# All DMA transposes issued by ScalarE instead of SyncE, and a new order of all instructions

## The chip, the cores and the metric

The kernel runs on one core of a Trainium2 chip. A core has five engines with a queue of instructions each: TensorE (PE, matmuls into PSUM), VectorE (DVE), ScalarE (ACT, activations and copies), GpSimd (POOL) and SyncE (SP, which here issues DMAs). They share on-chip memory (SBUF), and 16 DMA engines move the data. The queues run side by side and wait for each other on semaphores. A DMA is issued by an instruction in the queue of one engine. The metric is the time of one execution on the device in microseconds; the median of the runs counts.

## The reference

Attention with a choice of key chunks by bounds, then a gated MLP with a mix over the sequence (batch B = 4, heads H = 8, sequence S = 768, head size 64, model size 512, hidden size 1024):

```python
k_min, k_max = min and max of k over chunks of 32 keys
ub = sum_d max(q * k_min, q * k_max)              # bound of each (query, chunk)
ub = where(query's chunk >= chunk, ub, -1e9)
sel = the 6 chunks with the largest ub
scores = where(sel and key <= query, q @ k.T / 8, -1e9)
attn_out = softmax(scores) @ v                    # heads joined: x, (4, 768, 512)
h = gelu_tanh(x @ w_in);  u, v = halves of h
v_n = (v - mean) / sqrt(var + 1e-6) * g_ln
v_s = einsum('ts,bsd->btd', w_sg, v_n) + b_sg
out = x + (u * v_s) @ w_out
```

(The first, third and fourth lines are put shortly here.)

## The kernel before

The 32 heads go in 16 pairs, p = 0 to 15; four pairs make a batch b, and after its four pairs a batch goes through the MLP. Everything is unrolled, and every step is recorded by `P.op(engine, function, cost, tag, ...)` with what it reads and writes.

For each pair, `kside` (pairs 0 to 9) or `kside_full` (pairs 10 to 15) readies the keys. The first transposes the keys `kn` on PE and evicts them (`kev`) into `KA`. The second reduces `kn` to the chunk bounds on DVE (L580), casts the two heads of the pair into the tile `kbx` (`kcast`, POOL or ACT; for odd pairs this tile is `IND`, so that the page shows `kbx` and `IND`), and transposes each head by DMA into `KA` (`kT_p_i`, L587). `qside` transposes the queries on PE, evicts them to `qT` (`qev`), makes the positive part `rT` (`rel`) and casts `QA` (`qcast`). `vside` casts the values. `select` and `select_full` compute the bounds (`ub`), pick the chunks and write the mask `Dt`, which SP copies into `QA` (`qd`, L742). `scores` and `scores_full` multiply `KA` by `QA` into one of the two double banks `PSC` (`sc`, L778), and ACT takes the exponential into `E` (`exp_p_i_c`, L784, three pieces for each head). `head` multiplies `E` by the values (`pv`, `pvd`) and DVE scales the result into `XS` (`xs`, L873).

When two heads of `XS` are there, `xtrans(b, dk)` puts their transpose into `xT`: for batches 1 and 2 by DMA (`dt_x_b_dk`, L882), for 0 and 3 on PE with an eviction (`xev`). `moe_h` multiplies `xT` by `w_in`; ACT takes GELU into `vgb` (`gv`, L909) and `uT` (`gu`, L950); DVE takes statistics and forms `vhat`. `moe_g` mixes over the sequence (L962), gates on DVE, and multiplies by `w_out` (L981); DVE adds `XS` into `osb` and SP stores it (L992).

The exponential and GELU need different activation tables, so ACT's list has one block of GELUs for each batch, with a table load on each side.

The order on each engine is written out: `TABLE` holds, for each engine, the numbers of its recorded steps in the order in which they are issued, the PSUM bank of each tile (`slots`), and the engine of the steps that can go to more than one (`engine`, read into `ENG` by tag). The cost tuples, `dmac(1250)` for one, are a planner's, and the planner is not in the file; the emitted program does not depend on them. `place` puts the lists in place. `link` finds for each step the semaphore waits that its data needs and that no earlier step of the same engine has waited for. An engine issues in order, so that a step that waits holds all later ones of its list. A DMA in a list waits, is issued, and its landing raises a semaphore of its own.

In the kernel before every DMA is in SP's list (158 steps), the 20 transposes among them: 12 `kT` (pairs 10 to 15, two heads each) and 8 `dt_x` (batches 1 and 2, four each).

Of the kernel before, what the change touches and what calls it, by code (L numbers as in the profile page):

```python
# [261 lines left out]
def _build(nc, ctx, q, k, v, w_in, g_ln, w_sg, b_sg, w_out, out):  # L262
# [30 lines left out]
    P = Program()  # L293
# [47 lines left out]
    xT = [T(f"xT{i}", [128, NDK, S], BF16) for i in range(2)]  # L341
# [83 lines left out]
    ENG = dict(x.split(":") for x in TABLE["engine"].split())  # L425
# [68 lines left out]
    QRUN = [0] * 16  # L494
    KRUN = [0] * 16
# [80 lines left out]
    def kside_full(p, u, x):  # L576
# [7 lines left out]
        for i in range(2):  # L584
            flex("pool", ("act",), lambda i=i: kbx[n][:, i, :, 64 * i:64 * i + 64], lambda i=i: kn[s][:, i], TG + 60,
                 ("kcast", p, i), [("kn", s, 0), ("kn", s, 1), ("kbi", n, i)], [("kbx", n, i)])
            P.op("sp", lambda e, i=i: e.dma_start_transpose(  # L587
                KA[w][i][:].rearrange("p (t x) -> p t x", x=128), kbx[n][:, i].rearrange("p t c -> p (t c)")), dmac(1250),
                ("kT", p, i), reads=[("kbx", n, i), ("kbi", n, i)], writes=[("KA", w, i, 0), ("KA", w, i, 1), ("KI", w, i)],
                dma=f"kT{w}_{i}", xfer=900)  # L590
# [287 lines left out]
    def xtrans(b, dk):  # L878
        src = XS[:, b % 2, dk]
        rd = [("XS", b % 2, 2 * dk), ("XS", b % 2, 2 * dk + 1)]  # L880
        if (b, dk) in DXT:
            P.op("sp", lambda e: e.dma_start_transpose(xT[b % 2][:, dk, :].rearrange("p (t x) -> p t x", x=128),  # L882
# [3 lines left out]
        t = ps_g.tile((0, 1))  # L886
# [160 lines left out]
    for p in range(4, NP + 4):  # L1047
# [37 lines left out]
    "act": (  # L1085
# [10 lines left out]
    "dve": (  # L1096
# [17 lines left out]
    "pool": (  # L1114
# [12 lines left out]
    "slots": (  # L1127
        "23102213010323200101101110130011110010232110001110123120310010010032011111010102300110103332323232322232"
# [73 lines left out]
```

## Time and profile before

| | |
|---|---|
| runs of the kernel before | 220.44, 222.28, 221.87 us; median 221.87 |
| the profiled execution | 220.88 us, its span 218.8 us |
| granted TensorE clock | 1.000 |
| DMA | 36.27 MB in 98,235 packets, mean 166 GB/s |
| SP waiting | longest in total: L992 for DVE osb, 30.8 us in 10 times |

The span runs from the first to the last instruction. Busy time counts computing only: issuing a DMA is an instruction of its engine's queue, but not busy time. In a row of groups stand the line, engine, operation, output and inputs with the shape, the count, then the busy time and the mean ns of one, then the idle time just before and what ended it. In a row of waits stand the waiting engine, tile and line, what it waited for, and the total in us, the times and the longest. SPq is SP's queue.

### The profile page before, as it was taken

To read this page: it belongs to the slowest core of one execution; us is meant where nothing else is said; L and a number is where in the kernel's file an instruction comes from. 1 tells how busy PE (TensorE), PEld (TensorE's weight loads), DVE (VectorE), ACT (ScalarE), POOL (GpSimd) and SP (SyncE) were. 2 spreads that over 40 slices of the span, in tenths; PEclk is the share of its full clock that TensorE was granted. 3 is DMA by queue.
4 is the path that set the end of the run, shared out by engine and by line. 5 is a ranking of instruction groups with operands and counts; after the bars stand their busy time and mean duration, and the time that the engine had idled before them with its cause. 6 is when DMAs were issued, how large, how long until landed. Compare 5 with 4: busy or idle time off the path is not lost.

```text
span 218.8 us, 5980 instructions
## 1 busy us (share of the span) xinstructions
PE 199.7 (91%) x2363; PEld 131.0 (60%) x2377; DVE 187.1 (85%) x532; ACT 166.6 (76%) x251; POOL 93.5 (43%) x132
## 2 busy tenths in 40 slices
PE   7599999989999997987996999998898999999992
PEld 3366676846757575666563667776444668555550
DVE  4899999899999998898989988956888768968993
ACT  3979999988999999788879867987867788275000
POOL 7333946991359743346124443796114034002000
PEclk9999999999999999999999999999999999999999
DMA  7999999993999979896999798985944004001216
GB/s 153 252 220 216 212 241 349 345 226 71 223 223 259 215 180 248 190 151 126 178 176 227 178 217 126 236 128 76 182 103 115 3 0 147 3 0 48 96 61 230
DMA packets 98235, 36.27 MB, mean 166 GB/s; under 512 B 92448, under 2 KB 93216, under 8 KB 98208
## 3 DMA queue, kind: packets, MB, share of 16 engines
q1 hardware_dynamic: 98208, 35.89, 76.7%
q8 instruction: 19, 0.31, 0.6%
q14 instruction: 8, 0.07, 0.1%
HBM read 24.77 MB, written 6.29 MB: 142 GB/s over the span
## 4 chain that ended last, share of the span: by engine, by line
PE 55%; DVE 25%; DMA 9%; issue 3%; POOL 3%; SPq 2%; ACT 2%; DVEq 0%
PE PSG L962 15%; PE PSC L778 9%; PE PSG L981 8%; PE PSG L524 5%; PE PSG L856 4%; DVE vhat L933 4%; DVE Wall L563 3%; DVE stats L914 3%; DMA kn<-in_k_dram 3%; PE PSG L905 3%; PE PSG L945 2%; PE PSG L709 2%; DMA QA<-Dt 2%; DMA out_dram<-osb 2%; PE PSG L863 2%
## 5 line engine op out<-in xcount | busy, mean ns | idle before, releaser
L784 ACT ACTIVATE E<-PSC 128x1024 bf16<-128x1024 f32 (+1 forms) x72 | 62.7, 916 | 13.8 <-PE PSC L778 13.3
L778 PE MATMUL PSC<-QA,KA 128*128 128x128 bf16 (+2 forms) x336 | 36.5, 246 | 1.7 <-DMA QA<-Dt 1.3
L962 PE MATMUL PSG<-wsgT,vhat 128*128 128x384 bf16 x192 | 35.1, 326 | 3.2 <-DVE vhat L933 2.3
L789 POOL TENSOR_SCALAR_AFFINE_SELECT E<-E 128x768 bf16<-128x768 bf16 x24 | 20.8, 872 | 30.9 <-ACT E L784 30.9
L778 PEld LDWEIGHTS PSC<-QA,KA 128*128 128x128 bf16 x336 | 24.0, 98 | 11.5 <-ACT E L784 2.4
L962 PEld LDWEIGHTS PSG<-wsgT,vhat 128*128 128x128 bf16 x192 | 17.8, 98 | 14.8 <-ACT uT L950 2.2
L950 ACT ACTIVATE uT<-PSG 128x384 bf16<-128x384 f32 x32 | 15.5, 489 | 12.1 <-PE PSG L945 11.8
L945 PE MATMUL PSG<-xT,winb 128*128 128x384 bf16 x128 | 24.2, 327 | 0.0
L438 POOL CAST QA<-qT 64x768 bf16<-64x768 f32 (+1 forms) x24 | 20.6, 862 | 8.2 <-PE PSC L778 4.0
L905 PE MATMUL PSG<-winb,xT 128*128 128x512 bf16 x90 | 21.4, 379 | 2.0 <-issue 0.8
L563 DVE TENSOR_REDUCE Wall<-PSG 128x12 f32<-128x384 f32 x40 | 20.6, 542 | 2.9 <-PE PSG L524 2.8
L833 ACT ACTIVATE E<-PSC 128x1024 bf16<-128x1024 f32 (+1 forms) x24 | 21.1, 919 | 2.0 <-PE PSC L824 1.7
L968 DVE SCALAR_TENSOR_TENSOR PSG<-PSG,glnT,bsgbc 128x384 f32<-128x384 f32 x32 | 19.6, 617 | 3.4 <-PE PSG L962 2.8
L981 PE MATMUL PSG<-woutb,uT 128*128 128x512 bf16 x88 | 21.8, 379 | 0.4
L988 DVE TENSOR_TENSOR osb<-PSG,XS 128x512 f32<-128x512 f32 x24 | 16.0, 684 | 6.7 <-PE PSG L981 3.6
L909 ACT ACTIVATE vgb<-PSG 128x512 f32<-128x512 f32 x24 | 14.1, 597 | 9.5 <-PE PSG L905 9.4
L856 PE MATMUL PSG<-vx,E 128*128 128x65 bf16 x480 | 19.7, 194 | 0.9 <-DVE osb L988 0.9
L856 PEld LDWEIGHTS PSG<-vx,E 128*128 128x128 bf16 x480 | 17.6, 98 | 2.9 <-DVE osb L988 1.2
L920 POOL TENSOR_TENSOR rstd<-rstd,neghalf 128x6 f32<-128x6 f32 x4 | 5.3, 1329 | 31.9 <-DVE rstd L918 31.9
L873 DVE TENSOR_TENSOR XS<-PSG,rden 128x384 bf16<-128x384 f32 x32 | 17.6, 550 | 0.7
L972 DVE TENSOR_TENSOR uT<-PSG,uT 128x384 bf16<-128x384 f32 x32 | 17.5, 553 | 0.7
L438 POOL CAST vx<-vn 128x768 bf16<-128x768 f32 x16 | 14.0, 879 | 8.2 <-DMA vn<-in_v_dram 8.0
(106 smaller groups left out, 366.6 us busy)
## 6 DMA issues: line engine op xcount, KB each, us to landing
qn<-in_q_dram SPq DMA_DIRECT2D x32, 192.0 KB, 4.5
vn<-in_v_dram SPq DMA_DIRECT2D x16, 384.0 KB, 4.9
out_dram<-osb SPq DMA_DIRECT2D x24, 256.0 KB, 2.4
kn<-in_k_dram SPq DMA_DIRECT2D x20, 192.0 KB, 4.9
kn<-in_k_dram SPq DMA_DIRECT2D x6, 384.0 KB, 5.2
uT<-in_moe_w_sg_dram SPq DMA_DIRECT2D x4, 384.0 KB, 6.9
vgb<-in_moe_w_in_dram SPq DMA_DIRECT2D x3, 512.0 KB, 6.4
QA<-Dt SPq DMA_DIRECT2D x24, 36.0 KB, 2.3
```

Of the source, the lines that this page charges most:

```text
L438: return e.tensor_copy(dst(), src())
L563: P.op("dve", lambda d, m=m, op=op, t=t, hf=hf: d.tensor_reduce(W[w][:, m, 12 * hf:12 * hf + 12], t.ap()[:, 0:TG].rearrange("p (c x) -> p ...
L778: r = e.matmul(t.ap()[:, o:o + n], KA[w][i][:, 128 * kb:128 * kb + 128], QA[w][i][:, q0:q0 + n], start=True, stop=True)
L784: P.op("act", lambda e, t=t, c0=c0, c1=c1, i=i: e.activation(E[es][:, i, c0:c1], t.ap()[:, 0:c1 - c0], ACTF.Exp, scale=SCALE), act(c1 - c0 ...
L789: P.op("pool", lambda g, ev=ev: g.affine_select(ev, ev, pattern=[[0, NT], [1, 128]], compare_op=ALU.is_ge, fill=0.0, base=0, channel_multi ...
L833: P.op("act", lambda e, t=t, c0=c0, c1=c1, n=n: e.activation(E[es][:, :, c0:c1], t.ap().rearrange("p (i x) -> p i x", i=2)[:, :, 0:n], ACT ...
L856: r = e.matmul(t.ap()[:, 65 * qb:65 * qb + 65], E[es][:, i, a:a + 128], vx[w][:, kb, i, :], start=first, stop=False, skip_group_check=True)
L905: r = e.matmul(t.ap()[:, 0:F], xT[s][:, dk, 128 * qt:128 * qt + 128], winb[:, dk, F:DFF], start=(dk == 0), stop=(dk == NDK - 1))
L945: r = e.matmul(t.ap()[:, 0:TG], winb[:, dk, 128 * fb:128 * fb + 128], xT[s][:, dk, TG * tg:TG * tg + TG], start=(dk == 0), stop=(dk == NDK ...
L962: r = e.matmul(t.ap()[:, 0:TG], vhat[s][:, sb, 128 * fb:128 * fb + 128], wsgT[:, sb, TG * tg:TG * tg + TG], start=(sb == 0), stop=(sb == N ...
L968: P.op("dve", lambda d, t=t, fb=fb, tg=tg: d.scalar_tensor_tensor(t.ap()[:, 0:TG], t.ap()[:, 0:TG], glnT[:, fb:fb + 1], bsgbc[:, TG * tg:T ...
L981: r = e.matmul(t.ap()[:, 0:DM], gT[s][:, fb, 128 * qt:128 * qt + 128], woutb[:, fb, :], start=(fb == 0), stop=(fb == NF - 1))
```

## The change

The two kinds of transposes get their engine from `ENG` with `TENG = "act"` where it names none, and it names none: all 20 are issued by ACT. Every list of `TABLE` is new.

```diff
@@ -492,6 +492,7 @@
         P.op("sp", gln_load, dmac(), ("wg", 0), writes=["glnT"], dma="gln", xfer=300, bulk=NBULK)
 
     QRUN = [0] * 16
+    TENG = "act"
     KRUN = [0] * 16
 
     def load_rows(p, nm, src, dst, run):
@@ -584,7 +585,7 @@
         for i in range(2):
             flex("pool", ("act",), lambda i=i: kbx[n][:, i, :, 64 * i:64 * i + 64], lambda i=i: kn[s][:, i], TG + 60,
                  ("kcast", p, i), [("kn", s, 0), ("kn", s, 1), ("kbi", n, i)], [("kbx", n, i)])
-            P.op("sp", lambda e, i=i: e.dma_start_transpose(
+            P.op(ENG.get(f"kT_{p}_{i}", TENG), lambda e, i=i: e.dma_start_transpose(
                 KA[w][i][:].rearrange("p (t x) -> p t x", x=128), kbx[n][:, i].rearrange("p t c -> p (t c)")), dmac(1250),
                 ("kT", p, i), reads=[("kbx", n, i), ("kbi", n, i)], writes=[("KA", w, i, 0), ("KA", w, i, 1), ("KI", w, i)],
                 dma=f"kT{w}_{i}", xfer=900)
@@ -879,7 +880,7 @@
         src = XS[:, b % 2, dk]
         rd = [("XS", b % 2, 2 * dk), ("XS", b % 2, 2 * dk + 1)]
         if (b, dk) in DXT:
-            P.op("sp", lambda e: e.dma_start_transpose(xT[b % 2][:, dk, :].rearrange("p (t x) -> p t x", x=128),
+            P.op(ENG.get(f"dt_x_{b}_{dk}", TENG), lambda e: e.dma_start_transpose(xT[b % 2][:, dk, :].rearrange("p (t x) -> p t x", x=128),
                                                        src.rearrange("p t c -> p (t c)")), dmac(1250), ("dt_x", b, dk),
                  reads=rd, writes=[("xT", b % 2, dk)], dma=f"dtx{b % 2}_{dk}", xfer=900)
             return
...
```

The lists of numbers are long, so here is what they say. PE and the banks have a new order of the same work. These steps change their engine:

| from, to | steps |
|---|---|
| SP to ACT | the 20 transposes |
| ACT to DVE | kev_0_1, kev_9_0_0, kev_9_1_0, qev_3_0, qev_3_1, qev_5_0, qev_11_1, qev_12_1, qev_13_0, qev_14_0, qev_15_1, rel_11 to rel_14, vhat_0_2, vhat_1_0, vhat_3_2, wev_1_0, wev_1_1, xev_0_2 |
| ACT to POOL | kcast_10_1, kcast_13_0, kcast_13_1, mrow_0_1_0, qcast_3, qcast_4_0, qcast_11_0, wic_0, woc_2, woc_3 |
| DVE to ACT | qev_0_0, rel_0, rel_3, rel_4, rel_9, vhat_0_3, vhat_3_4, xev_0_1, xev_3_1, xev_3_2 |
| POOL to ACT | kcast_12_0, mrow_1_1_0, mrow_2_1_0, qcast_5_1 |

Of ACT's new list this is the part from the last exponential of pair 6 to the last of pair 15, by tags, the transposes in brackets, with the step that a transpose waits for where it has a wait of its own (the other 12 have none, since an earlier step of the list has waited for as much):

```
exp_6_1_1  [dt_x_1_0]  exp_7_0_0  [dt_x_1_1 <- xs_5_0]  exp_7_0_1  exp_7_1_1  qev_12_0  exp_7_0_2  exp_7_1_0
exp_7_1_2  [dt_x_1_2 <- xs_6_1]  qev_11_0  [dt_x_1_3 <- xs_7_1]  [kT_10_1]  exp_8_1_0  exp_8_1_2  gv_1_1
gv_1_0  [kT_10_0]  gv_1_2  gv_1_3  [kT_12_1 <- kcast_12_1]  gv_1_5  kcast_12_0 <- kT_10_0  gv_1_4  gu_1_0_1
[kT_11_1]  gu_1_0_0  gu_1_3_0  [kT_11_0]  gu_1_2_0  gu_1_3_1  qev_13_1  gu_1_1_0  qev_14_1  gu_1_2_1  gu_1_1_1
exp_8_1_1  exp_8_0_1  exp_8_0_0  exp_8_0_2  [kT_12_0]  exp_9_0_1  exp_9_0_0  exp_9_0_2  exp_9_1_2  [kT_13_0 <-
kcast_13_0]  exp_9_1_1  exp_9_1_0  [kT_13_1]  exp_10_0_0  exp_10_1_2  exp_10_1_1  exp_10_0_1  exp_10_0_2
[dt_x_2_0]  exp_10_1_0  exp_11_1_0  [kT_14_1 <- kcast_14_1]  exp_11_1_2  exp_11_0_0  exp_11_1_1  exp_11_0_1
[dt_x_2_1]  exp_11_0_2  exp_12_0_0  exp_12_0_2  [dt_x_2_2 <- xs_10_1]  exp_12_1_1  exp_12_0_1  exp_12_1_0
exp_12_1_2  [dt_x_2_3 <- xs_11_0]  exp_13_1_0  exp_13_1_1  exp_13_1_2  gv_2_0  gv_2_1  [kT_14_0]  gv_2_3
gv_2_2  [kT_15_1]  gv_2_5  gv_2_4  gu_2_2_0  gu_2_1_1  gu_2_0_0  gu_2_0_1  gu_2_3_0  gu_2_3_1  gu_2_2_1
gu_2_1_0  exp_13_0_2  exp_13_0_1  exp_15_1_0  exp_14_1_2  exp_14_0_1  exp_14_1_0  exp_14_1_1  exp_13_0_0
exp_14_0_2  [kT_15_0]  exp_15_1_2  exp_15_1_1  exp_14_0_0  exp_15_0_1  exp_15_0_0  exp_15_0_2
```

`kcast_12_0`, now on ACT, waits for the landing of `kT_10_0`. SP's list keeps its other 138 steps.

More of the change, by code (lines that the diff above doesn't have):

```diff
@@ L1069 @@
     "pe": (
[15 rows of a table removed]
-    "act": (
[10 rows of a table removed]
-    "dve": (
[17 rows of a table removed]
-    "pool": (
[12 rows of a table removed]
[15 rows of a table added]
+    "act": (
[10 rows of a table added]
+    "dve": (
[17 rows of a table added]
+    "pool": (
[12 rows of a table added]
     "slots": (
-        "23102213010323200101101110130011110010232110001110123120310010010032011111010102300110103332323232322232"
-        "33223222332301100032000000111023111101011010320110011032101010232332332233222333333222323210011033100111"
-        "10321001010111012311101000320101012323323332232223322233232233001110231001101321110010320100101231213003"
-        "2032111012311302030302"),
+        "03212312003223111111000010023303011010320102001101023130001110010123010011010103211101002223332323233223"
+        "22323332222311011023100000101032100010101011321101100123000101233223232223333332323232322210001122111000"
+        "11321101101011103210110000231010103223233222333232233322323332110001321001101230111010231100101320210320"
+        "2330011222003012313132"),
     "filler": (
-        "49:8 "),
+        "50:8 "),
     "engine": (
[7 rows of a table removed]
[8 rows of a table added]
 }
```

121 rows, old and new, of the table TABLE are left out of this document.

## The prediction

> **What bounds the kernel now.** I read the page's head first, then the busy time by stage, then the waits of TensorE (PE) and ScalarE (ACT), and last the chain of waits around the operations that move.
>
> ```profile
> span 218.8 us, 5980 instructions
> PE 199.7 (91%) x2363; PEld 131.0 (60%) x2377; DVE 187.1 (85%) x532; ACT 166.6 (76%) x251; POOL 93.5 (43%) x132
> ```
>
> PE is busy for 199.7 of 218.8 us, so no change of order can take away more than the other 19.1 us. ACT averages 76%, and that average hides the stage that matters. The next view cuts the span at 91.3 us, where ACT starts the first exponential of head pair 7, and at 185.5 us, where its last exponential ends. Columns are the length, the busy time of each engine, the granted clock, the DMA share (above 1 where the packets of an engine overlap) and GB/s.
>
> ```profile
> core 0: us, PE busy (x) PEld busy (x) DVE busy (x) ACT busy (x) POOL busy (x), PEclk, DMA share, GB/s
> 0.00:91.30 91.30, 83.51 (x1066) 57.07 (x1071) 83.44 (x248) 81.39 (x131) 53.21 (x84) 1.00 0.99 224
> 91.30:185.50 94.20, 86.87 (x1121) 57.92 (x1124) 77.70 (x232) 75.36 (x106) 38.69 (x47) 1.00 0.77 141
> 185.50:218.80 33.30, 29.34 (x186) 16.02 (x186) 25.97 (x54) 9.83 (x17) 1.61 (x2) 1.00 0.20 74
> ```
>
> In the middle stage PE has 7.3 us without work and ACT 18.8 us. Nearly all that ACT idles there is spent waiting for PE, so PE leads and ACT follows with some room:
>
> ```profile
> ACT E L784 <- PE PSC L778: 13.3, 19, 1.2
> ```
>
> All 20 transposes are issued at or near this stage (the first at 87.8 us, the last at 162.3 us), today by SyncE (SP), which computes nothing. Their rows (shortest, median and longest issue in ns) are the prices of this prediction:
>
> ```profile
> L587 SPq DMA_TRANSPOSE KA<-kbx x6: 1287/1341/2024, 103.5 to 155.4; - x6
> L587 SPq DMA_TRANSPOSE KA<-IND x6: 1237/1460/1904, 112.4 to 162.3; - x6
> L882 SPq DMA_TRANSPOSE xT<-XS x8: 1212/1308/1867, 87.8 to 151.0; - x8
> ```
>
> The chain of waits passes through them once in a way that costs something: SP issues a transpose, its landing frees a buffer, a key load follows, and VectorE (DVE) is kept from the vhat row that PE wants.
>
> ```profile
> 101.01 1.23 SPq L882
> ...
> 103.50 1.29 SPq L587
> 104.83 3.59 DMA KA<-kbx
> 108.48 0.52 POOL kbx L438
> 109.01 6.31 DMA kn<-in_k_dram
> 115.34 0.98 DVE Bn L580
> 116.57 2.38 DVE vhat L933 x5
> ```
>
> **What moves to ACT.** At the medians the 20 issues take 8 x 1.308 + 6 x 1.341 + 6 x 1.460 = 27.3 us, 1.36 each. What the new order takes off ACT, against this, I counted in the lists between the first exponential of pair 7 and the last of pair 15: one exponential fewer (it comes earlier), 5 fewer qT evictions (9 to 4), all 4 rT, one QA cast, one key cast of two and the one vhat row. Their rows (busy us, mean ns of one, idle before), with those of the two GELUs, which are used below:
>
> ```profile
> L784 ACT ACTIVATE E<-PSC 128x1024 bf16<-128x1024 f32 (+1 forms) x72 | 62.7, 916 | 13.8 <-PE PSC L778 13.3
> L950 ACT ACTIVATE uT<-PSG 128x384 bf16<-128x384 f32 x32 | 15.5, 489 | 12.1 <-PE PSG L945 11.8
> L909 ACT ACTIVATE vgb<-PSG 128x512 f32<-128x512 f32 x24 | 14.1, 597 | 9.5 <-PE PSG L905 9.4
> L435 ACT ACTIVATE qT<-PSG 128x384 f32<-128x384 f32 x28 | 13.1, 493 | 0.5 <-PE PSG L524 0.3
> L435 ACT ACTIVATE rT<-qT 128x576 f32<-128x576 f32 x10 | 6.9, 687 | 0.1
> L435 ACT ACTIVATE QA<-qT 64x768 bf16<-64x768 f32 x2 | 1.7, 838 | 0.0
> L435 ACT ACTIVATE IND<-kn 128x384 bf16<-128x384 f32 x2 | 1.0, 514 | 0.0
> L928 ACT ACTIVATE vhat<-vgb,nmr,rstd 128x512 bf16<-128x512 f32 x4 | 3.1, 811 | 0.3 <-DVE nmr L922 0.3
> ```
>
> By busy time over count (neighbours overlap) that is 0.87 + 5 x 0.47 + 4 x 0.69 + 0.85 + 0.50 + 0.78 = 8.1 us. The stage then holds 75.4 - 8.1 = 67.3 us of computing. With issues at full price it holds 94.6 us, which is the whole stage as it stands, 94.2 us.
>
> **How much of an issue ACT feels.** No row shows an issue on ACT, so it is bounded. Nothing is felt if activations already handed to the datapath cover it; the full 1.36 us each if ACT stands still. I rule out a gain from the issue itself, since ACT issues nothing now. I take a value between: ahead of the 20 transposes the new order has twelve exponentials, four vgb and two uT GELUs, one qT eviction and one other transpose, which hides nothing: (12 x 0.92 + 4 x 0.60 + 3 x 0.49) / 20 = 0.75 us. Half of it still running hides 0.37 us. So ACT feels 1.0 us, 20 us in all, and the demand is 67.3 + 20 = 87.3 us.
>
> How full can ACT be? It held 81.4 of 91.3 us (89%) in the first stage, where PE too was served. In its densest stretch it held more:
>
> ```profile
> 60.00:75.00 15.00, 14.62 (x134) 9.49 (x134) 14.68 (x27) 14.65 (x24) 12.02 (x17) 1.00 1.06 233
> 87.80:105.00 17.20, 14.91 (x295) 11.13 (x297) 15.35 (x52) 13.95 (x20) 7.45 (x10) 1.00 0.97 160
> 105.00:120.00 15.00, 13.06 (x109) 7.47 (x108) 13.45 (x46) 12.77 (x23) 4.21 (x6) 1.00 1.20 191
> ```
>
> That is 98%, for 15 us. Over 94 us I take 89%: 87.3 / 0.89 = 98.1 us, **+3.9 us**. The ends are 0 (at 98%, 87.3 fits into 89.1 us, and PE leads as before) and +12.1 us (the full price at 89%: 94.6 / 0.89 = 106.3).
>
> **Waits that come with the transposes.** Eight of the 20 carry a wait of their own: five on DVE's rows of XS, three on a GpSimd (POOL) cast. While ACT stands in such a wait, every exponential and GELU behind it in its list stands too, PE's score banks stay full, and PE stops at the next score. On SP the same waits cost loads at most:
>
> ```profile
> SPq L882 <- DVE XS L873: 5.2, 4, 3.0
> SPq L587 <- PE PSC L778: 3.8, 2, 2.0
> ```
>
> That is 9.0 us in six waits, 1.5 each. ACT comes later to its transposes, behind a fuller list, so I take **+1.0 us**, from 0 to 8 x 1.5 = 12. A key cast moved from POOL to ACT (pair 12) also waits for a transpose of pair 10 to land; three GELUs into vgb and a second issue stand between, so ACT reaches it 3 x 0.59 + 2 x 1.34 = 4.5 us after the first issue began. In the chain above the landing came 4.9 us after its issue began (103.50 to 108.42). I take nothing for it, and 0.4 at most.
>
> **What SP gives back.** Without 27.3 us of issues, the query, key and value loads, the mask rows into QA and the stores behind the transposes start earlier. What PE lost to such transfers in the stage bounds the gain:
>
> ```profile
> PE PSC L778 <- DMA QA<-Dt: 1.3, 1, 1.3
> PE PSG L905 <- DMA xT<-XS: 0.5, 1, 0.5
> ...
> PE PSG L962 <- DVE vhat L933: 1.9, 1, 1.9
> ```
>
> The last is the end of the chain above: 3.7 us in all. DMA engines are already at 0.97 and 1.20 where these waits lie, so an earlier issue shortens them only in part; I take **-1.5 us**, from 0 to -3.7.
>
> **The rest of the new order.** DVE takes over five qT evictions, four rT and the vhat row: 5 x 0.54 at its own price below, and 4 x 0.69 + 0.78 at ACT's, 6.2 us, so 83.9 of 94.2 us, a lower share than in the first stage; POOL, at 38.7 of 94.2 us, takes some casts. Neither leads; nothing, with -1 to +1 us for where the pieces fall. In the tail two of the four xT evictions go from DVE to ACT. ACT waits there anyway and the four are no longer in one line, which saves 4 x 0.55 - 2 x 0.81 = 0.6 us; I take **-0.5**, from -1 to +0.5. The table loads stay as many, eight.
>
> ```profile
> L438 DVE COPY qT<-PSG 128x384 f32<-128x384 f32 x4 | 2.2, 544 | 0.0
> L438 DVE COPY xT<-PSG 128x768 bf16<-128x768 bf16 x7 | 3.8, 549 | 0.2 <-PE PSG L890 0.2
> L435 ACT ACTIVATE xT<-PSG 128x768 bf16<-128x768 bf16 x1 | 0.8, 806 | 0.0
> ```
>
> Sum: 3.9 + 1.0 - 1.5 - 0.5 = +2.9 us on the profiled execution, 220.88 us (its span of 218.8 and 2.1 around it), so 223.8. The median of the runs, 221.87, lies 1.0 us above that execution; the median I forecast is **224.8 us**, in its own range 222.5 to 229.
>
> **Rivals.** *The issue is hidden and SP's relief counts (faster).* If ACT has two activations handed over when an issue begins, 2 x 0.75 us covers 1.36 us; ACT then holds 67.3 of 94.2 us, has more room than before, and what is left is -3.7 + -0.5 and some of ACT's relief: 221.9 - 3.5 to 4.5, about 218. For it: 13.3 us of ACT's waits are for PE, and a wait gives an issue its place. Against it: where ACT waits for PE nothing is queued that could run. It decides where less than 0.3 us is felt per issue. The Trainium skill (Perfetto Trace Analysis, "DVE / Act Engine Instruction") says that a sequencer pushes an activation into a wait queue and is at once ready to decode the next instruction, which is this rival's mechanism; no row here shows how many are queued.
>
> *Nothing changes.* The transfers are bound by the DMA engines (0.97 and 1.20), what ACT feels fits into its 18.8 idle us, and both terms vanish: 221.9. The Trainium skill (DMA: Bandwidth & Descriptors, "Issuing engines are not separate DMA queues") holds that a second issuing engine saves only the issuing time; the DMA shares agree.
>
> *ACT stands in the waits (much slower).* If it meets the waits as SP did, 9.0 us in place of my 1.0, its 18.8 idle us take little of it because ACT then idles at another place than PE: 224.8 + 8.0 = 232.8, and from 230 up. It decides where ACT reaches a transpose more than 1 us before its XS row or cast is done.
>
> A rule speaks against the change: by the same skill page on traces ("DMA Instruction — HWDGE (DVE, Sync)") an issuer locks a shared descriptor generator. If SP and ACT share it, each would wait out the other's issue; no row with two issuers exists here. As a mechanism of this kernel: a copy holds its issuer for 0.58 us in the row below; an issue on ACT that always met one half done would feel 20 x 0.29 = 5.8 us more, 93.1 us of demand, 93.1 / 0.89 = 104.6, which is 6.5 above the forecast's 98.1: 231.3. I give it 0.04, taken from within the waits' case below, since it ends beside it.
>
> ```profile
> 102.29 0.58 SPq L501 DMA_DIRECT2D qn<-in_q_dram  x1
> ```
>
> **How the numbers follow.** About 1% is what a measurement of this kernel can tell from no change; the three runs before spread by 0.8%. Faster means under 219.7, slower above 224.1. The forecast has 0.44: 0.34 slower, 0.10 within. The hidden issue has 0.30: 0.27 faster, 0.03 within. Nothing changed has 0.12: 0.06 within, 0.03 on each side. ACT standing still in front of a transpose, in the waits (0.10) or by the lock (0.04), has 0.14, all slower. Together 0.30 faster, 0.19 within, 0.51 slower. The range reaches from the middle of the hidden case's lower half, 217.0, to the lower end of the waits' case, 230; what is left out are the far ends of both, 0.17.
>
> **What would show it.** ACT's busy share in the middle stage should fall to about 67 us of computing, with gaps of about 1 us behind each issue, put down to no other engine. If gaps behind issues are under 0.3 us, the price is wrong. PE's waits for E on ACT, today not among its longest, should grow to several us; if not, ACT did not become the bound. PE's waits for QA and for vhat should shrink. Waits of ACT for XS or for the casts, of 2 us and more, would show the last rival. A changed first stage (91.3 us) would make the sum wrong where it takes nothing.

## The result and the profile after

The changed kernel ran in 233.91 us (median of 4, 233.18 to 234.51), the kernel before in 221.20 us beside it: a ratio of 1.0596, 95% interval 1.0541 to 1.0651. The forecast was 224.8 us, its range 217 to 230. The direction was right, the size was not, and the time lies above the range. The medians below are of all runs of a kernel, while its ratio leaves out runs over 1.5% above its fastest, since some executions of one kernel run slower than others.

The head of the page of the changed kernel:

```profile
span 232.3 us, 5989 instructions
...
PE 208.6 (90%) x2377; PEld 134.5 (58%) x2377; DVE 197.1 (85%) x543; ACT 159.1 (68%) x234; POOL 95.1 (41%) x138
```

DVE is busy 10.0 us longer than before, PE 8.9 us, ACT 7.5 us less. The place is found with an event that both kernels have: ACT's table loads. The load ahead of the first GELU block comes at 45.6 us before and at 55.3 us after, so 9.7 of the 13.5 us of span are lost there. The first transpose on ACT is issued at 98.11 us. The view by stages, cut at 20 us, at that table load and again 45.7 us later, first of the kernel before, then of the changed one:

```profile
20.00:45.60 25.60, 24.05 (x454) 17.62 (x452) 23.89 (x71) 24.46 (x34) 19.97 (x26) 1.00 1.09 285
45.60:91.30 45.70, 43.83 (x455) 29.73 (x459) 43.50 (x123) 42.03 (x74) 24.89 (x35) 1.00 0.87 199
```

```profile
20.00:55.30 35.30, 27.80 (x481) 21.18 (x475) 32.48 (x74) 24.24 (x33) 21.84 (x28) 0.90 0.86 221
55.30:101.00 45.70, 44.99 (x486) 30.70 (x494) 43.98 (x129) 42.30 (x73) 24.34 (x38) 1.00 0.85 189
```

In the first stretch PE idles 7.5 us (before 1.6) and runs at a granted clock of 0.90. DVE is busy for 92% of it with 3 instructions more than before, so something on DVE takes longer. The chain of waits of the changed kernel names it (start, us, what):

```profile
26.14 3.01 DVE Wall L574
...
39.83 5.65 DVE Wall L574
```

L574 (L573 before) is the step `wsub`: it subtracts two halves of `Wall`, 128 x 24 numbers, for each of the pairs 0 to 9. The view by source line, first before, then after (shortest, median, longest in ns):

```profile
L573 DVE TENSOR_TENSOR Wall<-Wall x10: 140/180/801, 9.0 to 90.9; 128x24 f32<-128x24 f32 x10
```

```profile
L574 DVE TENSOR_TENSOR Wall<-Wall x10: 140/174/5652, 8.1 to 100.1; 128x24 f32<-128x24 f32 x10
```

An instruction of 0.17 us takes 5.65 us, and another of the same line 3.09 us. PE waits behind them: the first and the third of these waits lie in this stretch. The second comes among the transposes and is taken up further down.

```profile
PE PSG L891 <- DVE qT L438: 3.8, 1, 3.8
...
PE PSC L779 <- DMA QA<-Dt: 3.3, 2, 2.9
...
PE PSG L663 <- DVE XS L874: 2.6, 1, 2.6
```

What runs on GpSimd in that time? The timeline of POOL in the changed kernel, and that of DVE. A row can hold neighbours of one kind together (x2 is two steps); it ends at its start plus its length:

```profile
38.64 0.87 POOL L841 TENSOR_SCALAR_AFFINE_SELECT E<-E 128x768 bf16<-128x768 bf16 x1
39.46 0.41 POOL L755 MEMSET QA<- 64x384 uint32 x1
39.82 1.03 POOL L438 CAST winb<-vgb 128x1024 bf16<-128x1024 f32 x1
40.80 1.68 POOL L841 TENSOR_SCALAR_AFFINE_SELECT E<-E 128x768 bf16<-128x768 bf16 x2
42.44 1.03 POOL L438 CAST winb<-xT 128x1024 bf16<-128x1024 f32 x1
43.42 2.02 POOL L438 CAST winb<-vgb 128x1024 bf16<-128x1024 f32 x2
```

```profile
39.25 0.56 DVE L438 CAST KA<-PSG 64x384 bf16<-64x384 f32 x1
39.83 5.65 DVE L574 TENSOR_TENSOR Wall<-Wall 128x24 f32<-128x24 f32 x1
45.49 0.56 DVE L438 COPY qT<-PSG 128x384 f32<-128x384 f32 x1
```

From 39.82 to 45.44 us each GpSimd step starts before the record of the one ahead has ended. The subtraction starts with the first and ends at 45.48, when GpSimd has nothing more to do. The other case (`wsub_3`, 26.06 us, 3.09 us) ends at 29.15, and GpSimd's line has its first gap from 29.11 to 29.18. The kernel before has the same kind of line, eight steps without a gap from 37.09 to 43.41 us, but there the subtraction had ended 0.06 us ahead of its first step. DVE's `xs`, with one input in PSUM and one in SBUF, keeps its usual 0.54 to 0.56 us beside that line. The rows (DVE, then POOL with the first and the last of the eight, both of the kernel before):

```profile
36.86 0.17 DVE L573 TENSOR_TENSOR Wall<-Wall 128x24 f32<-128x24 f32 x1
```

```profile
37.09 0.83 POOL L438 CAST vx<-vn 128x768 bf16<-128x768 f32 x1 [1.56 <-DMA vn<-in_v_dram]
...
42.81 0.60 POOL L410 TENSOR_SCALAR_AFFINE_SELECT kbx<-kbx 128x384 bf16<-128x384 bf16 x1
```

The theory put to the test: a DVE instruction with two inputs in SBUF is held while GpSimd runs, and with GpSimd's steps back to back it is held through all of them, until a gap. The Trainium skill (SBUF — State Buffer, "Who interferes with whom") says that such an instruction and a GpSimd instruction that reads SBUF share ports by an exclusive lock, and that whichever issues first blocks the other; the two rows of 3.09 and 5.65 us agree with a lock, and go on past the one instruction that it speaks of.

### The profile page after: what moved, and what is told of

Its sections match the earlier page's. It is cut to its first block, busy times and chain, and to the rows that moved or that the text cites. A ratio compares the mean times of both kernels' runs of the same rounds, so it can differ in the third digit from the quotient of the medians.

```text
span 232.3 us, 5989 instructions
## 1 busy us (share of the span) xinstructions
PE 208.6 (90%) x2377; PEld 134.5 (58%) x2377; DVE 197.1 (85%) x543; ACT 159.1 (68%) x234; POOL 95.1 (41%) x138
## 4 chain that ended last, share of the span: by engine, by line
PE 58%; DVE 15%; ACT 12%; DMA 4%; SPq 4%; issue 2%; POOL 2%; ACTq 1%; DVEq 0%; POOLq 0%
PE PSG L963 9%; PE PSC L779 8%; PE PSG L906 7%; PE PSG L946 7%; ACT E L785 6%; PE PSG L525 6%; PE PSG L857 5%; PE PSG L982 4%; DVE Wall L574 4%; DMA QA<-Dt 3%; PE PSG L663 3%; SPq L512 2%; PE PSG L710 2%; PE PSG L864 2%; PE PSC L819 2%
## 5 line engine op out<-in xcount | busy, mean ns | idle before, releaser
L779 PE MATMUL PSC<-QA,KA 128*128 128x128 bf16 (+2 forms) x336 | 37.3, 247 | 5.1 <-DMA QA<-Dt 3.3
L790 POOL TENSOR_SCALAR_AFFINE_SELECT E<-E 128x768 bf16<-128x768 bf16 x24 | 20.7, 864 | 30.6 <-ACT E L785 30.5
L438 POOL CAST QA<-qT 64x768 bf16<-64x768 f32 (+1 forms) x26 | 21.4, 826 | 15.0 <-ACT qT L435 13.1
L946 PE MATMUL PSG<-xT,winb 128*128 128x384 bf16 x128 | 23.7, 327 | 0.9 <-ACT uT L951 0.6
L906 PE MATMUL PSG<-winb,xT 128*128 128x512 bf16 x96 | 23.7, 390 | 0.2 <-ACT vgb L910 0.2
L982 PE MATMUL PSG<-woutb,uT 128*128 128x512 bf16 x96 | 23.5, 379 | 0.0
L857 PE MATMUL PSG<-vx,E 128*128 128x65 bf16 x480 | 20.7, 197 | 0.5 <-ACT E L785 0.4
L525 PE MATMUL PSG<-identF,qn 128*128 128x128 f32 x96 | 16.4, 288 | 2.2 <-DVE U L719 1.5
L915 DVE BATCH_NORM_STATS2 stats<-vgb 128x6 f32<-128x512 f32 x24 | 15.7, 678 | 3.1 <-ACT vgb L910 3.0
```

What stands on the lines that cost most here:

```text
L438: return e.tensor_copy(dst(), src())
L525: r = e.matmul(t.ap()[:, 128 * j:128 * j + 128], src[:].rearrange("p i t d -> p (i t d)")[:, 128 * x:128 * x + 128], identF[:], is_transpo ...
L779: r = e.matmul(t.ap()[:, o:o + n], KA[w][i][:, 128 * kb:128 * kb + 128], QA[w][i][:, q0:q0 + n], start=True, stop=True)
L790: P.op("pool", lambda g, ev=ev: g.affine_select(ev, ev, pattern=[[0, NT], [1, 128]], compare_op=ALU.is_ge, fill=0.0, base=0, channel_multi ...
L857: r = e.matmul(t.ap()[:, 65 * qb:65 * qb + 65], E[es][:, i, a:a + 128], vx[w][:, kb, i, :], start=first, stop=False, skip_group_check=True)
L906: r = e.matmul(t.ap()[:, 0:F], xT[s][:, dk, 128 * qt:128 * qt + 128], winb[:, dk, F:DFF], start=(dk == 0), stop=(dk == NDK - 1))
```

## The experiments

All times are medians; ratios are to the kernel before on the same chip.

| experiment | us | ratio, 95% interval | longest `wsub` in its profile, us |
|---|---|---|---|
| the change | 233.91 | 1.0596, 1.0541 to 1.0651 | 5.65 and 3.09 |
| issue only | 225.17 | 1.0134, 1.0070 to 1.0198 | 0.80 |
| order only | 232.95 | none given | 5.64 and 3.22 |
| both stalls out | 223.82 | 1.0094, 1.0051 to 1.0138 | 0.63 |
| both stalls out, issue on SP | 223.98 | 1.0098, 1.0058 to 1.0138 | 0.63 |
| two gaps | 223.66 | 1.0119, 1.0058 to 1.0179 | 0.64 |
| second stall out | 228.63 | 1.0338, 1.0250 to 1.0427 | 3.08 |
| first stall out | 223.86 | 1.0139, 1.0059 to 1.0220 | 0.64 |
| second gap elsewhere | 223.90 | 1.0165, 1.0067 to 1.0264 | 0.66 |
| gap one step later | 224.28 | 1.0174, 1.0091 to 1.0258 | 0.69 |
| gap three steps later | 231.66 | 1.0501, 1.0414 to 1.0588 | 5.64 and 1.87 |
| issue only, ACT relieved | 231.58 | 1.0375, 1.0293 to 1.0456 | 1.87 |
| tail only | 221.67 | 1.0008, 0.9968 to 1.0048 | 0.52 |

### Which half of the change costs the time

**Issue only.** The order of before, with the 20 transposes in ACT's list at the places where SP issued them in the profile of before.

```diff
-            P.op("sp", lambda e, i=i: e.dma_start_transpose(
+            P.op("act", lambda e, i=i: e.dma_start_transpose(
...
-            P.op("sp", lambda e: e.dma_start_transpose(xT[b % 2][:, dk, :].rearrange("p (t x) -> p t x", x=128),
+            P.op("act", lambda e: e.dma_start_transpose(xT[b % 2][:, dk, :].rearrange("p (t x) -> p t x", x=128),
```

> The order of the kernel before on every engine, with only the 20 transposes taken out of SP's list and put into ACT's, each behind the last ACT step that had started when SP issued it in the profile of before. Theory A (what was lost comes from the new order, above all from two small DVE subtractions that wait 3.0 and 5.6 us for GpSimd): within 2 us of before, 220 to 223. Theory B (the issue on ACT is the cost): most of the 12.7 us, 229 or more.

225.17 us: about 3 us over before. PE's waits of this kernel show the mechanism of the prediction, ACT late with its exponentials (before 0.3 us of such waits in the stage):

```profile
PE PSC L778 <- ACT E L784: 3.0, 5, 1.0
```

**Order only.** The new order, with the transposes back in SP's list.

```diff
-    TENG = "act"
+    TENG = "sp"
```

> The new order on every engine, with the 20 transposes given back to SP, each behind the last SP issue that had started when ACT issued it in the profile of the changed kernel. Theory A: the two long subtractions stay, 230 to 235. Theory B: 221 to 225.

232.95 us, from 228.38 to 234.36, with the same two stalls in its profile, which is of the run of 234.36 us. Four runs so far apart give no interval, but even the fastest lies 6.7 us above the kernel before, more than half of the change's 12.7 us. So most of the loss belongs to the order, whoever issues; the two experiments under the next heading say it more sharply.

### Taking the stalls away

**Both stalls out.** In the changed kernel the GpSimd step `aff_1_1` (261) also waits for `wsub_3` (171), and `aff_3_0` (377) for `wsub_4` (232). The numbers are those of the recorded steps. `aff` is GpSimd's selection on `E` (L841); below, `kbi` is its selection on `kbx` (L410), `wic` a cast into `winb` and `vcast` one of the values.

```diff
+        for late, early in ((261, 171), (377, 232)):
+            P.ops[late].deps.add(early)
```

> The changed kernel with two waits added on GpSimd: its selections aff_1_1 and aff_3_0 wait for the subtractions wsub_3 and wsub_4 on DVE, so that GpSimd stands still for a moment while each is due. Theory A: the two subtractions fall from 3.0 and 5.6 us to under 1 us each, the granted clock stays nearer to full between 40 and 60 us, and the time falls by 6 to 10 us, to 224 to 228. Theory B: no change beyond 2 us, 232 to 234.

**The same with the issue on SP.**

```diff
-    TENG = "act"
+    TENG = "sp"
...
+        for late, early in ((261, 171), (377, 232)):
+            P.ops[late].deps.add(early)
```

> Both edits on the new order: the two waits on GpSimd, and the 20 transposes back in SP's list. Against the run with the waits alone it prices the issuing engine on the new order. Theory A: within 2 us of that run, 222 to 228. Theory B: close to before, 221 to 223, and at least 5 us under the run with the waits alone.

223.82 and 223.98 us. Two waits give back 10.1 of the change's 12.7 us, and with the stalls gone it makes no difference which engine issues the transposes. The stretch up to the table load, of the kernel with both stalls out:

```profile
20.00:45.60 25.60, 24.55 (x472) 18.20 (x480) 24.56 (x73) 23.16 (x32) 21.91 (x28) 1.00 1.05 278
```

This is the order of the changed kernel, so the two rows can be set against each other: 35.30 - 25.60 = 9.7 us, of which PE idles 7.50 - 1.05 = 6.45 us more and is busy 27.80 - 24.55 = 3.25 us longer with the same work, at a granted clock of 0.90. By the starts of the subtractions, the changed kernel is 0.67 us late when the first stall begins (26.06 against 25.39), the stalls are longer by 3.09 - 0.63 and 5.65 - 0.63, 7.5 us in all, and 1.5 us come behind them. There the clock falls:

```profile
40.00:50.00 10.00, 5.47 (x96) 4.55 (x96) 9.47 (x12) 4.22 (x6) 5.45 (x6) 0.81 0.76 203
50.00:60.00 10.00, 9.43 (x94) 6.52 (x92) 7.90 (x29) 7.38 (x13) 5.30 (x9) 0.85 0.53 120
```

In single microseconds it is 1.00 up to 46 us and 0.50 from 47 to 52. With the stalls out both stretches hold 1.00. The Trainium skill (TensorE: Matmul & The Clock Gate, "HAM oscillation — how this bites in real kernels") warns of PE idle gaps over about 3.4 us; PE's wait of 3.8 us for `qT` above, just ahead of the fall, agrees. Shorter gaps show no sharp limit here: with the stalls out the clock was 0.50 from 103 to 106 us behind a wait of 2.8 us, and in the changed kernel it stayed at 1.00 behind the wait of 2.6 us for `XS`, which ended at 30.5 us.

**Is it the wait for the subtraction, or only a gap?** `aff_1_1` and `aff_3_0` wait for nothing but the GpSimd step just ahead of them in their own list.

```diff
+        for late, early in ((261, 389), (377, 77)):
+            P.ops[late].deps.add(early)
```

> The changed kernel, where aff_1_1 and aff_3_0 on GpSimd wait only for the GpSimd step just ahead of them to be finished, not for anything on DVE. If DVE is kept out because GpSimd runs its steps without a gap and takes the shared path anew each time, a gap of some tens of ns is enough: both subtractions under 1 us, and the time as with the waits on DVE, 222.5 to 225.5. If DVE is kept out for another reason (its own inputs, or a first-come order), the subtractions keep 3.0 and 5.6 us: 232 to 235.

223.66 us, the longest `wsub` 0.64 us. GpSimd's step ends at 25.82 in this profile and the next starts at 25.89: a gap of 0.07 us lets the subtraction through, no order between the two engines is needed.

### Which stall, and does its length follow the gap

**Second stall out only** (`aff_3_0` waits for `wsub_4`).

```diff
+        for late, early in ((377, 232),):
+            P.ops[late].deps.add(early)
```

> The changed kernel with one of the two waits: only aff_3_0 waits for wsub_4, so that the first subtraction (3.0 us) stays. If each long subtraction costs about its length, this run keeps some 2.5 to 3.5 us of the 10 that both waits gave back: 226 to 228. If the first is hidden behind other work, 223 to 225; if the whole loss hung on the first, 231 or more.

228.63 us (226.96 to 231.50): the stall left, 3.08 us long, costs 4 to 5 us, more than its length. Beside it on the same chip the kernel with two gaps took 223.66 us; the ratios, 1.0338 and 1.0119, differ by 4.8 us.

**First stall out only** (`aff_1_1` waits for `wsub_3`).

```diff
+        for late, early in ((261, 171),):
+            P.ops[late].deps.add(early)
```

> The changed kernel with the other one of the two waits alone: aff_1_1 waits for wsub_3, and wsub_4 keeps its 5.6 us. The run with only the second wait took 228.6, so that the first stall was worth 4.8 us and the second 5.3. If the two add up, this run takes 228.5 to 230; if the second hung on the first (a shift of GpSimd's backlog against DVE), wsub_4 shortens by itself and it takes under 226.

223.86 us, as with both out: the second stall is gone by itself. In this profile the cast ahead of `aff_3_0` ends at 37.57, `aff_3_0` waits for its exponential and starts at 37.68, and `wsub_4` gets through (POOL, then the line's view of DVE):

```profile
36.54 1.03 POOL L438 CAST winb<-vgb 128x1024 bf16<-128x1024 f32 x1
37.68 1.69 POOL L841 TENSOR_SCALAR_AFFINE_SELECT E<-E 128x768 bf16<-128x768 bf16 x2
```

```profile
L574 DVE TENSOR_TENSOR Wall<-Wall x10: 140/174/635, 7.9 to 89.8; 128x24 f32<-128x24 f32 x10
```

In the changed kernel that exponential ends at 40.49 and the cast at 40.85, so there is no wait and no gap. The first stall pushes the three engines apart by enough to make the second.

**Second gap at another place** (ahead of `wic_3`, 82, in place of `aff_3_0`).

```diff
+        for late, early in ((261, 389), (82, 378),):
+            P.ops[late].deps.add(early)
```

> As the run with the two gaps on GpSimd, but the second gap lies two GpSimd steps later: not aff_3_0 but wic_3, two selections further on, waits for the step ahead of it. If a DVE subtraction gets in at the first gap and only there, wsub_4 now lasts until that gap, two selections of 0.84 us longer: 2.3 to 2.8 us instead of 0.6, and the run takes 1 to 2.5 us more than with both early gaps, 224.5 to 226.5. If DVE gets in by waiting its turn, wsub_4 stays at 0.6 us and the time at 223.7.

223.90 us and a short `wsub_4`. That speaks neither for the theory nor against it: with the first stall gone the wait for the exponential makes the gap anyway, 0.12 us from 37.76 on. The length had to be tested at the first stall.

**Gap one step later** than the one that frees `wsub_3`, ahead of `kbi_0_0` (31).

```diff
+        for late, early in ((31, 261),):
+            P.ops[late].deps.add(early)
```

> The gap in GpSimd's line now stands not ahead of aff_1_1 but one step later, ahead of kbi_0_0 (27.20 us in the changed kernel). Theory A, the subtraction wsub_3 is held until the first gap between two GpSimd steps, however long those steps have run: it lasts from about 26.06 to 27.2 us, 1.1 to 1.3 us (0.64 with the gap ahead of aff_1_1, 3.09 with none). Theory B, any wait in GpSimd's list shifts its phase and so removes the stall by accident: 0.64 us as in the experiments with the earlier gap, or 3 us as if nothing had been changed. Time by A: the second stall decides; if it stays away as in the experiments on the first wait alone, 223.5 to 226 us; if it comes back, 229 to 234.

**Gap three steps later**, ahead of `vcast_1` (98).

```diff
+        for late, early in ((98, 34),):
+            P.ops[late].deps.add(early)
```

> The gap stands three steps later, ahead of vcast_1 (28.29 us in the changed kernel). Theory A: wsub_3 lasts from about 26.06 to 28.3 us, 2.1 to 2.4 us. Theory B: 0.64 or 3.09 us. Time by A: a longer first stall than in the kernel with the gap ahead of kbi_0_0, and so a time no shorter than that kernel's; 224.5 to 229 us without the second stall, 229 to 234 with it.

In the first of the two, `wsub_3` came at 25.05, ahead of a GpSimd copy at 25.21, and took 0.24 us, which is neither figure. The next DVE instruction with two SBUF inputs, the threshold into `Dn` (0.45 us in the changed kernel), was caught in its place, until the gap at 26.84 (DVE, then POOL):

```profile
25.21 1.94 DVE L686 TENSOR_TENSOR Dn<-U,m 128x288 bf16<-128x288 f32 x1
```

```profile
25.98 0.86 POOL L841 TENSOR_SCALAR_AFFINE_SELECT E<-E 128x768 bf16<-128x768 bf16 x1
26.90 1.24 POOL L410 TENSOR_SCALAR_AFFINE_SELECT kbx<-kbx 128x384 bf16<-128x384 bf16 x2
```

In the second, `wsub_3` took 1.87 us instead of 2.1 to 2.4, and the threshold behind it 0.90 us, up to 28.19; GpSimd's gap was from 27.89 to 27.95:

```profile
25.50 1.87 DVE L574 TENSOR_TENSOR Wall<-Wall 128x24 f32<-128x24 f32 x1
27.29 0.90 DVE L686 TENSOR_TENSOR Dn<-U,m 128x288 bf16<-128x288 f32 x1
```

So DVE was held for 1.5 us with the gap at 26.84 and for 1.7 + 0.45 = 2.1 us with the gap at 27.89, against 0.4 to 0.5 with the earliest gap and 2.9 with none: the loss goes with the place of the gap. But the rule is not sharp. At 27.35 the subtraction got in between two GpSimd steps whose records overlap, a kind of place that let nothing through at 27.79 in the changed kernel. The kernel before has such a place too: there a subtraction was held for one step only and ended at 23.04 us, though the next step's record begins at 22.96 (POOL, then DVE):

```profile
22.42 0.59 POOL L410 TENSOR_SCALAR_AFFINE_SELECT kbx<-kbx 128x384 bf16<-128x384 bf16 x1
22.96 0.82 POOL L438 CAST QA<-qT 128x768 bf16<-128x768 f32 x1
```

```profile
22.64 0.40 DVE L573 TENSOR_TENSOR Wall<-Wall 128x24 f32<-128x24 f32 x1
```

So each gap seen here let DVE in, and without one it was let in at some places and not at others; what decides that stays open. The times follow whether the second stall returns. With 1.5 us it does not (224.28 us, expected 223.5 to 226); with 2.1 us it does, 5.64 us long (231.66 us, expected 229 to 234).

### Two terms of the prediction by themselves

**ACT relieved.** The kernel with the issue alone, with `rel_11` to `rel_14`, four `qev` and one `vhat` on DVE, as in the new order.

```diff
+    ENG.update(rel_11="dve", rel_12="dve", rel_13="dve", rel_14="dve", qev_13_1="dve", qev_14_1="dve", qev_14_0="dve", qev_15_1="dve", vhat_1_0="dve")
```

> The order of the kernel before with the issues on ACT, as run already (225.2), and nine ACT steps beside the issues given to DVE: rel_11 to rel_14, qev_13_1, qev_14_0, qev_14_1, qev_15_1 and vhat_1_0, 5.5 us of ACT's time. If the 3 us that the issues cost there come from ACT being too full beside them, 1 to 2.5 us come back: 222.5 to 224. If they come from each issue standing in one place ahead of a step that PE needs, nothing changes (224.5 to 226); if DVE becomes the bound, over 226.

231.58 us: slower than the issue alone, where 222.5 to 224 was expected if ACT was too full, and over 226 if DVE became the bound. In its profile, of the slowest of the six runs, PE waits 3.7 us for `vhat` on DVE and still 4.9 us for exponentials, and a `wsub` is held for 1.87 us. The nine steps stand in DVE's list at other places than in the new order, so this says that these places were bad, and nothing on the term.

**Tail only.** The kernel before with `xev_3_1` and `xev_3_2` on ACT.

```diff
+    ENG.update(xev_3_1="act", xev_3_2="act")
```

> The kernel before, transposes on SP, with two of the four last evictions (xev_3_1 and xev_3_2) given from DVE to ACT, as the new order has them. The prediction's term: 0.5 us less (0.2 to 1.2), 220.5 to 221.5 beside 221.7. If the 1.3 us by which the changed kernel's tail is shorter come from its order and not from this, no change.

221.67 against 221.17 us: no change, within 0.5% either way.

## Why the prediction came out as it did

**The step that failed** is "The rest of the new order", where the prediction had "nothing, with -1 to +1 us for where the pieces fall". By the experiment with both stalls out it cost 10.1 us, nearly all of it in a stage that the prediction left out because no transpose is issued there: of the 11.0 us between the spans of the two kernels 9.7 lie ahead of the first GELU block. The step added up engines' busy time by stage and took each instruction's duration as fixed. A duration of DVE, though, depends on what GpSimd does at that moment, and the kernel before shows it: the same subtraction takes 140 ns and 801 ns there, and the one of 801 ns ends with a GpSimd copy that ran all the while (POOL, then DVE):

```profile
44.43 1.09 POOL L438 COPY KA<-INDF 64x768 bf16<-64x768 bf16 x1
```

```profile
44.75 0.80 DVE L573 TENSOR_TENSOR Wall<-Wall 128x24 f32<-128x24 f32 x1
```

The spread within one form was in view and was not asked about. The prediction's last line of "what would show it", that a changed first stage would make the sum wrong, is what came true: up to the first exponential of pair 7 it was 91.3 us before and is 100.7 us after.

**ACT fuller, +3.9 us.** In the new order this came to nothing: with the stalls out the issue on ACT and on SP gave 223.82 and 223.98 us. Cut as the prediction cut it, from the first exponential of pair 7 to the end of the last, the stage is 98.2 us long after, where 98.1 was foretold, and ACT computes for 68.3 us in it, where 67.3 was. But with the stalls out it is 97.7 us with the issue on ACT and 97.9 on SP (the changed kernel, then the one with the issue on SP):

```profile
100.66:198.83 98.17, 89.99 (x1108) 57.11 (x1108) 80.50 (x239) 68.28 (x92) 39.80 (x50) 0.98 0.71 134
```

```profile
90.70:188.57 97.87, 90.36 (x1101) 58.53 (x1108) 81.05 (x239) 68.91 (x92) 39.22 (x50) 0.97 0.67 134
```

So the longer stage comes with the order and not with the issue, and that its length was met is luck. The prediction's own sign says the same: PE's waits for exponentials came to 1.6 us after and not to several, so ACT did not become the bound.

In the old order the issue alone cost about 3 us (1.3%, interval 0.7 to 2.0%), with PE's waits for exponentials grown to 3.0 us, as the mechanism has it. That this is near 3.9 is luck too. There ACT is not relieved of the 8.1 us, and the prediction's sum would give (75.4 + 20) / 0.89 = 107.2 us, 13.0 us more than the stage's 94.2. The price was too high in both orders.

The price per issue was forecast at 1.0 us felt. The view of ACT's queue after (shortest, median, longest ns):

```profile
L588 ACTq DMA_TRANSPOSE KA<-kbx x6: 1226/1321/1474, 112.4 to 170.9; - x6
L588 ACTq DMA_TRANSPOSE KA<-IND x6: 1227/1262/1793, 124.9 to 191.3; - x6
```

```profile
L883 ACTq DMA_TRANSPOSE xT<-XS x8: 1227/1338/2497, 98.1 to 165.1; - x8
```

Summed over their single records the 20 issues take 28.0 us, and ACT computes during 14.5 us of that; 13.5 us, 0.67 each, are uncovered. ACT's timeline shows both ways:

```profile
98.11 1.36 ACTq L883 DMA_TRANSPOSE xT<-XS  x1
98.26 0.49 ACT L435 ACTIVATE KA<-PSG 64x384 bf16<-64x384 f32 x1
98.78 1.02 ACT L785 ACTIVATE E<-PSC 128x1024 bf16<-128x1024 f32 x1
```

```profile
141.16 0.70 ACT L785 ACTIVATE E<-PSC 128x640 bf16<-128x640 f32 x1 [0.55 <-PE PSC L779]
141.17 1.25 ACTq L588 DMA_TRANSPOSE KA<-IND  x1
142.58 1.02 ACT L785 ACTIVATE E<-PSC 128x1024 bf16<-128x1024 f32 x1 [0.71 <-PE PSC L779]
```

Where activations were handed over, two of them ran under the issue. Where the last one had waited for PE, the issue started with it and half of it was bare. Gaps of about 1 us were foretold; 0.67 lies between that and the 0.3 at which the rival of the hidden issue was to decide. The rival in which two issuers wait for each other put 0.29 us on an issue that meets one of SP's: the 14 issues that overlap one took a median of 1.33 us, the other six 1.27.

**Waits that come with the transposes, +1.0 us.** No such wait is among ACT's listed waits, for XS or for the casts; the rival in which ACT stands in them did not happen, though the time fell near its 232.8. A time that fits a rival is not the rival's mechanism.

**What SP gives back, -1.5 us.** Only in part. PE's wait for `vhat` shrank (1.9 us before, 0.2 after), that for QA grew: 3.3 us after, 1.3 before. With the stalls out it is still 3.0 us, 2.8 of it in one place. The chain of that kernel:

```profile
98.59 0.66 DVE Dt L738
99.25 0.02 issue
99.27 3.43 DMA QA<-Dt
...
102.75 1.57 PE PSC L779 x10
```

SP takes the mask's copy 0.02 us after DVE has it ready, so a less loaded SP can't help here: the mask itself is late, and PE stands for 2.8 of the transfer's 3.4 us.

**Tail, -0.5 us.** Not shown. After the last table load the changed kernel takes 32.0 us and before took 33.3, but the kernel with the tail's edit alone takes 31.3 there and no less time in all: evictions that move to ACT go ahead of that table load, and shift the mark. From the end of the last exponential on, where the prediction cut, it is 33.5 us after and 33.3 before.

**What stays open** is the last 1%: the new order with its stalls taken out is 2 us slower than before, with either issuer, and its stage of the transposes is 97.7 us long against 94.2. With the issue on ACT the QA wait above is 1.7 us longer than before and lies in that kernel's slow stretch:

```profile
95.00:105.00 10.00, 6.21 (x95) 4.74 (x99) 7.82 (x24) 4.82 (x8) 1.91 (x3) 0.88 1.20 176
```

This is read from the trace; no experiment has taken that wait away. No kernel tried here beats the one before.

## What to carry to other kernels

When a change moves the whole order, look at the rows whose duration spreads within one form (here 140 to 801 ns) and ask which other engine sets it, before adding up busy time by stage. A small DVE instruction with two inputs in SBUF should not begin inside a long line of GpSimd steps without a gap; two waits of GpSimd on its own preceding step, the first a gap of 0.07 us, were enough here to save 10 us. And a stall early on can line up the next one, so take out the first and look again.

## What the runs showed of the hardware that was not expected

- GpSimd's steps, back to back, kept DVE out for 5.65 us over six steps in one piece, not for one step at a time; gaps of 0.06 to 0.12 us ended such stalls. At some places it also got in where the records show no gap (27.35 us in the kernel with the gap three steps later, 23.04 us in the kernel before).
- Behind PE's idle gap of 3.8 us the granted clock was 0.81 in one stretch of 10 us and 0.85 in the next, with PE busy 94% in the second. With the stalls out it fell to 0.50 behind a gap of 2.8 us as well.
- Issues of DMA transposes on ACT took what they took on SP (medians 1.26 to 1.34 us, before 1.31 to 1.46), and up to two activations ran under one.
